# Division on GpSimd one slot later, with four rows of numerators and reciprocals, in an attention and MLP kernel

## The chip, the cores and the metric

The kernel runs on one core of a Trainium2 chip. The metric is the device time of one execution in microseconds (us). The profiled execution is one such run, and its trace names the instructions of each engine: PE (TensorE matmuls), PEld (its weight loads), DVE (VectorE), ACT (ScalarE), POOL (GpSimd) and SP (SyncE, which here only issues DMAs).

## The reference

```python
def _attn_ref(q, k, v, w_phi):
    def phi(x):
        proj = np.einsum('bhsd,df->bhsf', x, w_phi)
        proj = proj - np.max(np.abs(proj), axis=-1, keepdims=True)
        return np.concatenate([np.exp(proj), np.exp(-proj)], axis=-1)
    q_p, k_p = (phi(q), phi(k))
    kv = np.einsum('bhsf,bhsd->bhfd', k_p, v)
    z = np.sum(k_p, axis=2)
    num = np.einsum('bhsf,bhfd->bhsd', q_p, kv)
    den = np.einsum('bhsf,bhf->bhs', q_p, z)[..., None] + 1e-06
    return (num / den).astype(np.float32)

def _moe_ref(x, w_in, w_out, alpha):
    h = x @ w_in
    g = np.maximum(h, 0.0) + alpha * np.minimum(h, 0.0)
    return (g @ w_out).astype(np.float32)
```

The attention has 8 batches of 8 heads, 576 positions and 64 dimensions. Its output, turned to 4608 tokens by 512, goes through the two matrix products of the MLP (512 to 2048 to 512). All is float32.

## The kernel before

The first third of the run is the attention. Two heads make a pair, and there are 32 pairs. `places(i)` (L61) gives every step of pair i a time in slots, counted from slot i; all steps of all pairs are sorted by that time, and the order is kept on each engine's queue (PE, SP, DVE, ACT and POOL). So one slot of the steady state holds the late steps of one pair, the middle steps of the next, the early steps of those behind them, and the decoding of one block of the MLP's weights.

The steps around the change, with the place in slots of an ordinary pair i:

- `k_sum` (i + 0.0055, L406 and L407, POOL): two additions that make `y`, from which PE takes the sum of the key features in `k_z` (i + 1.0035, L433).
- `num` and `den` (i + 2.0013 and i + 2.004, PE, L522 and L541) read the exponentials of the queries, `qf`, which ACT wrote at i + 1.39 to 1.46 (L507, L510). ACT copies the numerators to a row `s` (i + 2.002, L534) and the denominators to `ds` (i + 2.0065, L551).
- `den_out` (i + 2.025, SP, L555) reads `ds` back in a small layout; `invert` (i + 2.7825, DVE, L559) takes the reciprocals; `rec_out` (i + 2.785, SP, L562) writes them to DRAM; `spread` (i + 3.027, SP, L567) reads them back, broadcast over the partitions, into a row `r`. It can only be issued when the write has landed.
- `finish` (i + 3.1, POOL, L572) multiplies `s` by `r`, and `store` (i + 3.8, SP, L575) writes the product to `x_d`, the input of the MLP.

The decoding of a weight block (`stages`, L178 to L239) runs between them: SP loads `raww` (L182), ACT scales (L191, L193), DVE takes the sign and joins (L200, L204), POOL adds (`decode_add`, L208), ACT halves (L148), DVE subtracts (L151) and SP stores (L238, L239). On POOL one slot is thus `y`, `y`, `finish`, add. On SP one slot is: the weight stores, `den_out`, `spread`, the weight load, the load of v (L329), the load of q and k (L325), `rec_out`, `store` of the pair before.

Buffers: `qf` has two of 9216 bytes per partition (`QH_BUFS`); `s` rotates among two in the pool `st` and one in `wk`; `r` has two in `st`. For the first four pairs ACT and DVE split the quotient into two parts (`first_x`, L657, at X0T + i), which are the first operands of the MLP.

After the last pairs (time T2, L723) the order by hand holds for PE, SP and POOL alone. The MLP's first column of tokens follows, then pairs of columns by a fast product with seven multiplications, in which `g_tiles` (L953) takes the two `qf` buffers for its units 0 and 1.

Of the kernel before, what the change touches and what calls it, by code (L numbers as in the profile page):

```python
# [8 lines left out]
F32 = mybir.dt.float32  # L9
# [8 lines left out]
P = 128  # L18
B, H, S, D = 8, 8, 576, 64
# [4 lines left out]
NPAIR = B * NP  # L24
# [8 lines left out]
C2 = 512  # L33
# [19 lines left out]
X_BUFS = 2  # L53
RAW_BUFS = 2
S_BUFS = 2
QH_BUFS = 2
NHALF = 1
NBURST = 3

# [1 line left out]
def places(i):  # L61
    end = i >= NPAIR - 2
    first = {}
    if i < NBURST:
        first = dict(
            ld=-1.9, lv=-0.45, p=(-0.9955, -0.2197), pl=-1.034 if i == 2 else -0.2217, ke=(-0.1643, -0.0202), y=0.0055
        )
    if i == 0:
        first |= dict(
            kz=0.965, ka=0.6934, ko=0.967, kr=1.1197, kc=1.4241, s0=1.9, s=1.91,  # L70
            d=1.77, ds=1.78, n=1.8361, q=(0.96, 0.9362, 0.4904), qe=(0.9994, 1.0, 0.968),
        )
    if i == 1:
        first |= dict(y=0.1, ka=0.003, kz=0.12, ko=0.43, kr=1.002)
    return dict(
        ld=-2.217,
        lv=-1.96,
        p=(-0.2197, -0.219),
        pl=-0.2185,
        dr=-0.218,  # L80
        ke=(-0.19, 0.0046),
        kz=1.0035,
        ka=1.0012,
        ko=1.0045,
        kr=1.0191,
        kc=1.1461,
        q=(1.4089, 1.41 if i == NPAIR - 1 else 1.4543, 1.3558),
        qe=(1.4364, 1.4627, 1.3892),
        d=2.004,
        ds=2.0065,  # L90
        n=2.0013,
        s0=2.002,
        s=2.0043,
        d9=2.025,
        dv=2.7825,
        rd=2.785,
        rr=3.027,
        x=6.75 if end else 3.1,
        xs=6.76 if end else 3.8,
        y=0.0055,  # L100
    ) | first


W = dict(load=-1.9212, sign=-0.1262, scale=-0.1512, split=-0.1196, add=-0.1112, high=0.8388, low=0.8674, store=1.0588)
W0 = dict(load=-1.3, sign=-0.9513)
X0T = 4.47
X0L = 0.363
HEADS = (31.9, 32.3, 32.62, 32.9)
T2 = 33.05
# [17 lines left out]
def fused_kernel(ctx: ExitStack, tc: tile.TileContext, kq, v, w_phi, w_in, w_out, alpha, out):  # L127
# [155 lines left out]
    qp = ctx.enter_context(tc.tile_pool(name="qp", bufs=2))  # L283
    wdq = ctx.enter_context(tc.tile_pool(name="wdf", bufs=2))
    st = ctx.enter_context(tc.tile_pool(name="st", bufs=2))
# [14 lines left out]
    wk = att.enter_context(tc.tile_pool(name="wk", bufs=3))  # L300
# [12 lines left out]
    for n in range(2):  # L313
        k4 = cat.tile([P, 2, 2, FD], F32, name=f"k4_{n}")
        pool.memset(k4[64:P], 0.0)
        k4buf.append(k4)

    def attention_units(i):
        b, hp = divmod(i, NP)
        c = {}  # L320
# [180 lines left out]
        def q_exp(h):  # L501
            ps = None if halved and h == 2 else c["qt", h]
            if h == 2:
                c["qf"] = qp.tile([P, 2, 2, S], F32, tag="qf", name=f"qf{i}", bufs=QH_BUFS)
            for a, sg in enumerate((1.0, -1.0)):
# [23 lines left out]

        def num_out(u):  # L530
            if u == 0:
                own = i % 3 == 2 and i < NPAIR - 2
                c["s"] = (wk if own else st).tile([P, S], F32, tag="s", name=f"s{i}", bufs=1 if own else S_BUFS)
            act.copy(c["s"][:, u * HS : (u + 1) * HS], c["n", u])  # L534

        def den():
# [25 lines left out]
            nc.sync.dma_start(rec_d[i].rearrange("(p j) -> p j", j=36), c["d9"])  # L562

        def spread():
            c["r"] = st.tile([P, S], F32, tag="r", name=f"rr{i}", bufs=2)
            for h in range(2):
                nc.sync.dma_start(  # L567
                    c["r"][h * D : (h + 1) * D], rec_d[i : i + 1, h * S : (h + 1) * S].broadcast_to([D, S])
                )
# [4 lines left out]
        def store():  # L574
            nc.sync.dma_start(x_d[hp, :, b * S : (b + 1) * S], c["r"])  # L575

        at = places(i)
        us = [
            (at["ld"], load),
# [7 lines left out]
            (at["n"], num),  # L587
            (at["d"], den),
            (at["s0"], lambda: num_out(0)),
            (at["s"], lambda: num_out(1)),  # L590
            (at["ds"], den_copy),
            (at["d9"], den_out),
            (at["dv"], invert),
            (at["rd"], rec_out),
            (at["rr"], spread),
            (at["x"], finish),
            (at["xs"], store),
# [39 lines left out]
    xs, po = {}, {}  # L637
# [19 lines left out]
    def first_x(j, rows):  # L657
# [8 lines left out]

        return [(X0T + j, cast), (X0T + X0L + j, rest)]

# [12 lines left out]
    def down_tile(name, dtype):  # L681
        return wdq.tile([P, 2, 2, WN], dtype, tag="wd", name=name, bufs=2 * NPRE)
# [237 lines left out]
    end = t1 + (len(order) - HEAD) * U2 - 0.002  # L920
# [30 lines left out]
        dve.scalar_tensor_tensor(g, r, al1[:, ff : ff + 1], src, op0=ALU.mult, op1=ALU.add)  # L951

    def g_tiles(p, u):  # L953
        if u < 2:
            t = qp.tile([P, 2, 2, S], F32, tag="qf", name=f"g_{p}_{u}", bufs=QH_BUFS)
            return {(r, c): t[:, r, c, :C2] for r in range(2) for c in range(2)}
        if u < 4:
            t = [down_tile(f"g_{p}_{u}_{r}", F32).rearrange("p c t w -> p c (t w)") for r in range(2)]
            return {(r, c): t[r][:, c] for r in range(2) for c in range(2)}
        if u == NU - 1:  # L960
            tag = lambda r, c: (st, [P, S], "sr"[r])
        else:
            tag = lambda r, c: (late["gs"], [P, C2], f"g{u}{r}{c}")
        g = {}
        for r in range(2):
            for c in range(2):
                q, shape, t = tag(r, c)
                g[r, c] = q.tile(shape, F32, tag=t, name=f"g_{p}_{u}_{r}{c}", bufs=2 if u == NU - 1 else 1)[:, :C2]
        return g
# [3 lines left out]
    def unit(p, u):  # L973
# [17 lines left out]
        def rest():  # L991
            g = g4[p, u] = g_tiles(p, u)
            if fresh:
                added(g[0, 0], st["b"], st["p1"])
            leaky(g[0, 0] if fresh else st["b"], g[0, 0], f1, f"11_{tag}")
            product(st["a"], p, u, S2, False, False)
            st["u2"] = copied(st["a"], f"u2_{tag}")
            st["c"] = bank(1, f"pc{tag}")
            product(st["c"], p, u, S1, True, False)
            p5 = copied(st["c"], f"p5_{tag}")  # L1000
            product(st["a"], p, u, S3, False, False)
            added(g[1, 1], st["a"], p5)
# [196 lines left out]
```

## Time and profile before

| | us |
|---|---|
| runs, not profiled (3): median | 989.25 |
| their lowest and highest | 985.78, 989.32 |
| the profiled execution | 985.83 |
| its span, first to last instruction | 984.0 |
| PE busy | 958.2 (97%) |
| DVE busy | 758.2 (77%) |
| ACT busy | 632.9 (64%) |
| POOL busy | 255.3 (26%) |

The shares are means over two very different parts. Up to about 310 us the attention keeps PE, DVE, ACT, POOL and the DMA engines all busy; from about 360 us to the end the MLP is a stream of matmuls. POOL's 255 us lie almost all in the first part. The granted clock of TensorE is 1.00 of full speed in every slice.

### The profile page before, as it was taken

What the parts mean: (1) busy time and instruction counts of PE and PEld (TensorE: products, weight loads), DVE (VectorE), ACT (ScalarE), POOL (GpSimd) and SP (SyncE); (2) the same over time, 40 slices, a digit from 0 to 9 for tenths busy, and PEclk for the clock granted to TensorE, in tenths of its full rate; (3) what the DMA queues carried; (4) which work ended last, traced back from release to release, by engine and by line L of the source; (5) the groups of instructions that cost most, each with busy time, mean ns of one, the idle gap of its engine ahead of it and who ended that gap; (6) DMA issues with size and microseconds to landing.
All of it is one profiled execution on the core that took longest, in us unless ns stands there. A gap on an engine that the chain in (4) does not pass through costs nothing.

```text
span 984.0 us, 19065 instructions
## 1 busy us (share of the span) xinstructions
PE 958.2 (97%) x7152; PEld 787.0 (80%) x7152; DVE 758.2 (77%) x1186; ACT 632.9 (64%) x1207; POOL 255.3 (26%) x222
## 2 busy tenths in 40 slices
PE   8999999989998999999999999999999999999998
PEld 6766667666675888888888888888888888888887
DVE  6899988887887499788988366987465986565874
ACT  5998989988887456566665455664445664454653
POOL 3567667666666122111001000000000000000001
PEclk9999999999999999999999999999999999999999
DMA  5688888988885789997778566677567676566565
GB/s 196 230 275 309 297 298 321 298 300 308 299 290 207 272 312 379 338 343 275 248 240 259 202 205 242 243 252 259 195 213 248 224 261 231 183 213 204 182 226 180
DMA packets 97611, 252.23 MB, mean 256 GB/s; under 512 B 12464, under 2 KB 13104, under 8 KB 97520
## 3 DMA queue, kind: packets, MB, share of 16 engines
q1 hardware_dynamic: 87088, 215.42, 64.8%
q0 software_dynamic: 10000, 35.39, 9.4%
q8 instruction: 57, 0.93, 0.4%
q14 instruction: 34, 0.28, 0.1%
q10 hardware_dynamic: 432, 0.20, 0.1%
HBM read 189.87 MB, written 60.96 MB: 255 GB/s over the span
## 4 chain that ended last, share of the span: by engine, by line
PE 61%; DVE 3%; DMA 2%; issue 1%; ACT 1%; POOL 0%; SPq 0%; ACTq 0%; DVEq 0%; POOLq 0%
PE qa L931 6%; PE qa L932 6%; PE qa L930 6%; PE pa L930 5%; PE pa L932 5%; PE pa L931 5%; PE qc L931 3%; PE qc L932 3%; PE qc L930 3%; PE pc L932 3%; PE pc L930 3%; PE pc L931 3%; PE qb L930 1%; PE qb L932 1%; PE qb L931 1%; PE pb L932 1%
## 5 line engine op out<-in xcount | busy, mean ns | idle before, releaser
L144 ACT CAST hv<-g 128x512 fp32r<-128x512 f32 x224 | 136.4, 619 | 91.7 <-PE qa L932 45.3
L154 DVE TENSOR_TENSOR hv<-g,hv 128x512 fp32r<-128x512 f32 x224 | 150.4, 685 | 40.3 <-ACT hv L144 39.1
L808 POOL DMA_DIRECT2D out_dram<-pt x35 | 18.9, 541 | 500.6 <-ACT pt L1098 429.3
L932 PE MATMUL qa<-hv,wv 128*128 128x512 f32 (+1 forms) x257 | 97.3, 379 | 0.0
L931 PE MATMUL qa<-hv,wv 128*128 128x512 f32 (+1 forms) x257 | 97.3, 379 | 0.0
L930 PE MATMUL qa<-hv,wv 128*128 128x512 f32 (+1 forms) x257 | 97.3, 379 | 0.0
L406 POOL TENSOR_TENSOR y<-xk 128x1024 f32<-128x1024 f32 x32 | 76.2, 2380 | 10.1 <-ACT xk L400 10.1
L400 ACT ACTIVATE xk<-t 128x1024 f32<-128x1024 f32 (+1 forms) x66 | 64.3, 1025 | 8.5 <-DVE t L386 8.5
L572 POOL TENSOR_TENSOR rr<-s,rr 128x576 f32<-128x576 f32 x32 | 49.5, 1548 | 75.5 <-DMA rr<-rec_d 36.7
L950 ACT ACTIVATE r<-g 128x512 f32<-128x512 f32 x65 | 37.4, 621 | 44.4 <-DVE g L946 44.4
L522 PE MATMUL n<-qf,sf 128*64 128x288 f32 x464 | 61.5, 407 | 2.9 <-DVE t L386 2.9
L419 PE MATMUL kv<-xk,v 128*64 128x256 f32 x512 | 62.3, 386 | 0.7 <-ACT ks L443 0.7
L385 DVE TENSOR_REDUCE m<-pj 128x8 f32<-128x1024 f32 (+2 forms) x38 | 43.2, 1136 | 25.1 <-PE pj L375 25.1
L510 ACT ACTIVATE qf<-qt 128x512 f32<-128x512 f32 x116 | 60.6, 639 | 0.0
L951 DVE SCALAR_TENSOR_TENSOR g<-r,al,g 128x512 f32<-128x512 f32 x65 | 45.9, 747 | 18.8 <-ACT r L950 18.8
L932 PEld LDWEIGHTS qa<-hv,wv 128*128 128x128 f32 x257 | 48.7, 190 | 6.8
L931 PEld LDWEIGHTS qa<-hv,wv 128*128 128x128 f32 x257 | 48.7, 189 | 6.8
L930 PEld LDWEIGHTS qa<-hv,wv 128*128 128x128 f32 x257 | 48.7, 189 | 6.7
L522 PEld LDWEIGHTS n<-qf,sf 128*64 128x64 f32 x464 | 34.0, 137 | 24.6 <-ACT aw L191 4.9
L154 DVE TENSOR_TENSOR xo<-xr,xo 128x512 fp32r<-128x512 f32 x56 | 40.5, 736 | 15.0 <-ACT xo L144 14.7
L144 ACT CAST xo<-xr 128x512 fp32r<-128x512 f32 x56 | 33.8, 619 | 25.7 <-DVE xr L859 12.6
L986 ACT COPY pb<-pa 128x512 f32<-128x512 f32 x31 | 17.7, 570 | 50.6 <-PE pa L932 50.0
(210 smaller groups left out, 2713.3 us busy)
## 6 DMA issues: line engine op xcount, KB each, us to landing
wv<-vs_d SPq DMA_DIRECT2D x64, 512.0 KB
ws<-us_d SPq DMA_DIRECT2D x54, 512.0 KB
wv<-v_d SPq DMA_DIRECT2D x48, 512.0 KB
wa<-u_d SPq DMA_DIRECT2D x37, 512.0 KB
raw<-kq_dram SPq DMA_DIRECT2D x31, 576.0 KB
v<-v_dram SPq DMA_DIRECT2D x32, 320.0 KB
rr<-rec_d SPq DMA_DIRECT2D x64, 144.0 KB
x_d<-rr SPq DMA_DIRECT2D x32, 288.0 KB
```

Source lines behind the costliest of these rows:

```text
L144: return act.copy(dst, src)
L154: return eng.tensor_tensor(dst, src, f(hi), op=ALU.subtract)
L400: act.activation(x[:, a, :, js], c["t", 0][:, :, js], AF.Exp, scale=sg)
L406: pool.tensor_tensor(y, x[:, :, : 2 * FD], x[:, :, 2 * FD :], op=ALU.add)
L419: pe.matmul(c["kv"][h * D : (h + 1) * D, 0:2], lhsT=c["v"][:, tp, h, :], rhs=c["x", ch][:, :, h, j, :], start=tp == 0, stop=tp == NV - 1,)
L510: act.activation(dst, ps, AF.Exp, scale=sg)
L522: pe.matmul(ps[h * D : (h + 1) * D, :], lhsT=c["st"][:, a, h * D : (h + 1) * D], rhs=c["qf"][:, h, a, u * HS : (u + 1) * HS], start=a == 0 ...
L572: pool.tensor_tensor(c["r"], c["s"], c["r"], op=ALU.mult)
L930: pe.matmul(ps, lhsT=wh, rhs=xh, start=first, stop=False, skip_group_check=True)
L931: pe.matmul(ps, lhsT=wl, rhs=xh, start=False, stop=False, skip_group_check=True)
L932: pe.matmul(ps, lhsT=wh, rhs=xl, start=False, stop=end, skip_group_check=True)
L951: dve.scalar_tensor_tensor(g, r, al1[:, ff : ff + 1], src, op0=ALU.mult, op1=ALU.add)
```

## The change

The division of a pair moves from i + 3.1 to i + 4.1 and its store from i + 3.8 to i + 4.8, for all but the last two pairs. The broadcast read moves from i + 3.027 to i + 3.05, which on SP puts it behind the weight load (slot fraction 0.03) and the load of v (0.04). The splits for the first four pairs move one slot later (X0T). Since a row now lives a slot longer, numerators and reciprocals have four rows each: two in `st` and two single tiles in the pool `qp`, which take the room of the second `qf` buffer. In the MLP unit 1 of `g_tiles` uses these four rows.

```diff
-QH_BUFS = 2
+QH_BUFS = 1
@@ def places(i):
-        rr=3.027,
-        x=6.75 if end else 3.1,
-        xs=6.76 if end else 3.8,
+        rr=3.05,
+        x=6.75 if end else 4.1,
+        xs=6.76 if end else 4.8,
@@
-X0T = 4.47
+X0T = 5.47
@@ def fused_kernel(...):
+    def row(kind, i):
+        if i % 4 > 1:
+            return spare(f"{kind}{i % 4}", f"{kind}{i}")
+        return st.tile([P, S], F32, tag=kind, name=f"{kind}{i}", bufs=2)
+
+    def spare(tag, name):
+        return qp.tile([P, S], F32, tag=tag, name=name, bufs=1)
@@ def num_out(u):
-                own = i % 3 == 2 and i < NPAIR - 2
-                c["s"] = (wk if own else st).tile([P, S], F32, tag="s", name=f"s{i}", bufs=1 if own else S_BUFS)
+                c["s"] = row("s", i)
@@ def spread():
-            c["r"] = st.tile([P, S], F32, tag="r", name=f"rr{i}", bufs=2)
+            c["r"] = row("r", i)
@@ def g_tiles(p, u):
+        if u == 1:
+            return {(r, c): spare(f"{'sr'[r]}{2 + c}", f"g_{p}_{u}_{r}{c}")[:, :C2] for r in range(2) for c in range(2)}
```

## Rows read from the trace of the kernel before

**Rows 1.** Windows, three stretches: length, busy us (instructions) by engine, clock, DMA share, GB/s.

```profile
40.00:100.00 60.00, 57.73 (x816) 40.28 (x816) 57.48 (x83) 56.10 (x118) 42.89 (x26) 1.00 0.84 288
100.00:300.00 200.00, 187.48 (x2708) 132.11 (x2702) 172.03 (x256) 177.17 (x380) 134.26 (x84) 1.00 0.88 302
300.00:363.00 63.00, 60.16 (x367) 47.85 (x358) 43.37 (x66) 34.65 (x71) 23.49 (x24) 1.00 0.72 256
```

**Rows 2.** Groups by line, POOL, 99 to 310 us: busy us, mean ns | idle before.

```profile
L406 POOL TENSOR_TENSOR y<-xk 128x1024 f32<-128x1024 f32 x22 | 52.4, 2384 | 0.0
L572 POOL TENSOR_TENSOR rr<-s,rr 128x576 f32<-128x576 f32 x23 | 35.5, 1544 | 64.9 <-DMA rr<-rec_d 29.6 <-DVE ew L200 12.4 <-DVE aw L204 7.8
L407 POOL TENSOR_TENSOR y<-y 128x512 f32<-128x512 f32 x23 | 29.7, 1291 | 1.8
L208 POOL TENSOR_TENSOR aw<-cw,aw 128x512 int32<-128x512 int32 x22 | 28.0, 1273 | 2.0 <-ACT qf L510 2.0
```

**Rows 3.** Waits, 100 to 310 us, of PE (all) and ACT's longest: total, times, longest.

```profile
PE kv L433 <- POOL y L407: 10.4, 12, 2.0
PE n L522 <- DVE t L386: 1.3, 1, 1.3
PE m L375 <- ACT qf L507: 0.6, 1, 0.6
...
ACT raww L148 <- POOL aw L208: 15.7, 16, 2.2
```

**Rows 4.** Timeline of PE, the first matmuls on `y` of some pairs: start, us.

```profile
99.53 0.43 PE L433 MATMUL kv<-y,ones 128*32 128x128 f32 x8 [0.25 <-POOL y L407]
...
126.73 0.43 PE L433 MATMUL kv<-y,ones 128*32 128x128 f32 x8 [0.33 <-POOL y L407]
137.05 0.43 PE L433 MATMUL kv<-y,ones 128*32 128x128 f32 x8 [1.44 <-POOL y L407]
145.85 0.43 PE L433 MATMUL kv<-y,ones 128*32 128x128 f32 x8
...
288.31 0.42 PE L433 MATMUL kv<-y,ones 128*32 128x128 f32 x8
298.94 0.43 PE L433 MATMUL kv<-y,ones 128*32 128x128 f32 x8 [1.76 <-POOL y L407]
```

**Rows 5.** Timeline of POOL, 205 to 216 us.

```profile
205.04 1.87 POOL L572 TENSOR_TENSOR rr<-s,rr 128x576 f32<-128x576 f32 x1 [4.61 <-DMA rr<-rec_d]
206.88 1.28 POOL L208 TENSOR_TENSOR aw<-cw,aw 128x512 int32<-128x512 int32 x1
...
215.15 1.41 POOL L572 TENSOR_TENSOR rr<-s,rr 128x576 f32<-128x576 f32 x1 [3.31 <-DMA rr<-rec_d]
```

**Rows 6.** Timeline of SP, DMA issues, 197 to 214 us.

```profile
197.05 0.60 SPq L555 DMA_DIRECT2D d<-ds  x1
...
203.75 0.33 SPq L562 DMA_DIRECT2D rec_d<-d  x1
206.94 0.33 SPq L575 DMA_DIRECT2D x_d<-rr  x1
...
210.44 1.67 SPq L567 DMA_DIRECT2D rr<-rec_d  x2
...
213.78 0.37 SPq L562 DMA_DIRECT2D rec_d<-d  x1
```

**Rows 7.** Timeline of DVE, ACT and POOL, single rows.

```profile
203.35 0.37 DVE L559 RECIPROCAL d<-d 32x36 f32<-32x36 f32 x1 [2.25 <-DMA rr<-rec_d]
204.95 0.69 DVE L204 SCALAR_TENSOR_TENSOR aw<-aw,ew 128x512 uint32<-128x512 uint32 x1
213.65 0.39 ACT L551 ACTIVATE ds<-m 128x288 f32<-128x288 f32 x1
...
262.82 1.43 POOL L572 TENSOR_TENSOR rr<-s,rr 128x576 f32<-128x576 f32 x1 [3.55 <-DMA rr<-rec_d]
263.06 1.74 DVE L204 SCALAR_TENSOR_TENSOR aw<-aw,ew 128x512 uint32<-128x512 uint32 x1
```

## The prediction, made before the change was built

> **What bounds the kernel now.** I read four views in this order. The windows first: in the attention's steady part, 100 to 300 us, PE is busy 187.48 of 200 us, ACT 177.17, DVE 172.03 and POOL only 134.26 [rows 1]. By busy time POOL looks like the engine with most room, and that is the trap of this case.
>
> Second, the groups of POOL. Of its four steps per slot only the division waits: 64.9 us of idle time stand before its 23 instances, next to nothing before the others [rows 2]. Per slot POOL works 2.384 + 1.291 + 1.544 + 1.273 = 6.49 us and waits 64.9 / 23 = 2.82 us before the division, together 9.31 us. (The releaser is the broadcast read; the DVE lines named with it can't be, since the division reads only `s` and `r`.)
>
> Third, the slots by PE: the first matmul on `y` comes at 99.53 and, 21 slots later, at 298.94 [rows 4]. That is 9.50 us per slot. POOL's 9.31 us nearly fill it: POOL is never free, though a third of its time is waiting.
>
> Fourth, the waits show who pays. PE waits 10.4 us for `y`, and ACT 15.7 us for POOL's addition of the decoded weights; PE's other waits are 1.3 + 0.6 us [rows 3]. The queue on POOL is in order, so the division's wait is handed to `y` and to the addition behind it.
>
> The wait is also a loop. The division that starts at 205.04 ends at 206.91; SP then issues its store at 206.94 [rows 5, 6]. Behind that store on SP stand the weight stores, the denominators' read and the next broadcast, issued at 210.44, whose data releases the next division at 215.15 [rows 5, 6]. One turn is 215.15 - 205.04 = 10.11 us. The broadcast has a second condition, the landing of the reciprocals written at 203.75, 6.69 us before [rows 6].
>
> What would the slot be without POOL? A slot in which PE waits for nothing on `y` is 145.85 - 137.05 = 8.80 us [rows 4]; I take 8.81, to which several others come within 0.02. The excess of the 21 slots is 199.41 - 21 x 8.81 = 14.4 us. After 300 us PE has 63.00 - 60.16 = 2.8 us idle up to 363 us, and between 40 and 100 us it has 2.3 [rows 1].
>
> **The change, part by part.**
>
> *The division one slot later.* The count of instructions stays. The division now multiplies by a row that was issued almost a slot before: it is released when the second `y` ends. POOL's slot falls from 9.31 to 6.49 us of work, 2.3 below PE's 8.81. The addition behind it goes at the end of DVE's join instead of the end of the division: at 204.95 + 0.69 = 205.64 instead of 206.88 [rows 5, 7], 1.24 us earlier in this slot, and `y` with it. With POOL no longer a queue late, that grows until `y` waits for nothing but its exponentials.
>
> *The store one slot later.* SP issues it when the division is long done, so the weight stores, the denominators' read and what is behind them no longer wait for POOL. In the slot shown the store could be issued right after the reciprocals' write at 203.75 instead of at 206.94 [rows 6], so the denominators' read comes up to 3 us earlier for DVE.
>
> *The broadcast behind two loads.* It passes the weight load and the load of v on SP. These no longer stand behind its wait for the reciprocals, and SP's loop from one write of reciprocals to the next (213.78 - 203.75 = 10.03 us, of which 6.69 are the landing [rows 6]) loses their issue time. The broadcast now also stands behind v's wait for its buffer. It took 215.15 - 210.44 = 4.71 us to release the division [rows 5, 6]; behind two loads it may take several more, but it now has a whole slot more, 8.8 us. Cost: nothing; if that cover were gone, the division would wait again, for the overshoot.
>
> *One buffer of query exponentials.* ACT may write the next pair's `qf` only when PE's `num` and `den` have read the last. On ACT the copy of the denominators (at 213.65 [rows 7]), which needs `den` finished, stands before these exponentials in the same slot, so the wait is already met. Cost: nothing, and if ACT did wait, it would be no longer than this copy waits now. The rows of `s` and `r` come round after four slots and are held for under three. The casts of the first four pairs move with the division; unit 1 of `g_tiles` takes the new rows long after the last store. No cost.
>
> *The end of the attention.* Pair 29's division falls behind T2; it stays before the next DMA issue on POOL and after the last addition, which therefore no longer waits for the broadcast. PE has only 2.8 us idle there [rows 1]. I bound this part by -2 and +2.8 us and take 0, since PE is 95% busy; between 40 and 100 us DVE is busy 57.48 of 60 us, so I take 0 there also, with 2.3 us as the other end [rows 1].
>
> *The sum.* Excess 14.4 us, less PE's waits that have nothing to do with POOL (1.9 us [rows 3]): 12.5 us gained. Against the profiled execution this is 985.83 - 12.5 = 973.3 us. The median of the runs lies 989.25 - 985.83 = 3.4 us above that execution, so 976.8 us. What is late next is PE itself, with ACT at 177.17 / 200 x 9.50 = 8.4 and DVE at 8.2 us per slot close behind [rows 1]; their jitter can eat some. I put the gain of this case at 8 to 15 us.
>
> **A rule against the change.** A division that runs beside DVE's join makes the join 1.74 us instead of 0.69 [rows 7], 1.05 us more. The Trainium skill, GPSIMD Engine Reference, section 8 (Key points), says that GpSimd shares its SBUF interfaces with VectorE and contends with instructions that have two SBUF inputs; the trace agrees, 1.74 against 0.69. By that page the place of the division against DVE's three such steps (L151, L200, L204) decides, and the rival below is what it would do here.
>
> **The rivals.**
>
> *B. The round trip stays the bound.* Five of the 21 slots take over 10.3 us, from the one that ends at 137.05 (10.32) to the one that ends at 298.94 (10.63) [rows 4]; together they are 53.8 us, 9.8 above the floor. In one of them the denominators' read, issued at 197.05, holds DVE's reciprocal until 203.35, 6.30 us later, with 2.25 us of idle time on DVE [rows 6, 7]. If these trips and not POOL make the long slots, they stay: the gain is 12.5 - 9.8 = 2.7 us, 986.5 us. Against it: the read was late because the store before it stood behind the division. By the Trainium skill (DMA: Bandwidth & Descriptors, Anatomy of one DMA) a small transfer takes about 2.0 us, and this rival would be gone; the rows show 6.30 and 6.69 us, and they decide.
>
> *C. All goes to the floor*, the stretch from 40 to 100 us too: 14.4 + 2.3 = 16.7 us, 972.5 us. For it: the division beside DVE's steps also lengthens that stretch. Against it: DVE is nearly full there.
>
> *D. Slower: the division lands on DVE's steps.* DVE works 172.03 / 200 x 9.50 = 8.17 us per slot [rows 1]. If POOL's new order puts `y` or the division beside two of the three steps in each slot, DVE comes to 8.17 + 2 x 1.05 = 10.27 us: 21 x (10.27 - 9.50) = 16 us more, 1005 us. It decides from 9.50 - 8.17 = 1.33 us of stretch per slot on. Against it: the division would start right after `y`, some 5 us after the join (1.27 of addition and 3.68 of `y` [rows 2]) and end at 6.5, while the next three steps begin about 2 us before the next join at 8.8.
>
> *E. It doesn't do what it says:* the broadcast, behind two loads, lands after the `y` of the next slot, and POOL waits as before. No change, 989 us. It needs 4.71 + 8.8 = 13.5 us or more from issue to release, where 4.71 were seen.
>
> **How the numbers follow.** Forecast 0.62, B 0.16, C 0.07, D 0.07, E 0.08. The predicted time is the forecast's, 976.8 us. The range goes from 970.5 (C with 2 us from the end of the attention) to 987.0, just past B's centre; it leaves out D, E and a part of B. About 0.5% (5 us) is what a measurement of this kernel can tell from no change. Faster: forecast, C and a little of B, 0.72. Within: the rest of B, and E, 0.21. Slower: D, 0.07.
>
> **What would show each step.** In the profile after: the division's idle time before it goes from 64.9 to under 5 us; PE's wait for `y` and ACT's for the addition nearly vanish; SP issues the store with no wait for POOL; the first matmuls on `y` come 8.8 to 9.0 us apart, the long slots gone; DVE's join keeps 0.69 us. B would show as reciprocals or broadcasts that still wait for landings over 6 us, with slots over 10 us left; D as L151 and L204 well over 1 us; E as idle time before L572 that stays. A forecast that fails otherwise would have PE at 8.8 in the attention and the gain given back between 300 and 363 us.

## The result, and the profile after

The changed kernel takes 973.35 us (median of 4 runs, 969.33 to 974.84) against 988.08 us before (4 runs, 985.78 to 989.32): a ratio of 0.9847 with a 95% interval of 0.981 to 0.9885, or 14.7 us. Run again beside three others it gave 0.9863 (0.9839 to 0.9888). The forecast was 976.8 us, with a range of 970.5 to 987.0. The profiled execution took 972.53 us, with a span of 970.7 us; the one of before took 985.83 us with 984.0.

The windows of the changed kernel, with the columns of [rows 1] (length, busy us of PE, PEld, DVE, ACT and POOL with instructions, clock, DMA share, GB/s):

```profile
40.00:100.00 60.00, 60.00 (x875) 42.20 (x873) 56.39 (x87) 58.58 (x128) 41.88 (x27) 1.00 0.98 306
100.00:300.00 200.00, 197.97 (x2781) 139.81 (x2778) 175.62 (x261) 183.20 (x395) 141.97 (x90) 1.00 0.97 314
300.00:363.00 63.00, 60.43 (x298) 50.68 (x296) 47.81 (x84) 33.60 (x65) 17.05 (x25) 1.00 0.80 279
```

PE is busy 197.97 of 200 us where it was 187.48, and all of the 60 us before that. The DMA engines, at 0.88 before, are now at 0.97.

POOL's groups from 99 to 310 us, as [rows 2] (L579 is now the division):

```profile
L414 POOL TENSOR_TENSOR y<-xk 128x1024 f32<-128x1024 f32 x22 | 52.5, 2384 | 0.0
L579 POOL TENSOR_TENSOR r<-s,r 128x576 f32<-128x576 f32 x24 | 35.3, 1472 | 1.5 <-DMA r<-rec_d 1.5
L208 POOL TENSOR_TENSOR aw<-cw,aw 128x512 int32<-128x512 int32 x24 | 31.3, 1303 | 58.4 <-ACT qf L515 38.1 <-ACT qf L518 16.7 <-PE qt L457 2.1
L415 POOL TENSOR_TENSOR y<-y 128x512 f32<-128x512 f32 x22 | 28.5, 1295 | 1.7
```

The idle time before the division fell from 64.9 to 1.5 us. POOL still stands idle for 58 us, now before the addition, which needs DVE's join (the exponentials `qf` named in the row are not an input of it). That idle time is room: nobody waits for it, as the waits of 100 to 310 us show (total, times, longest):

```profile
DVE d L566 <- DMA d<-ds: 6.2, 6, 1.9
...
ACT raww L148 <- POOL aw L208: 2.7, 6, 0.5
...
PE kv L441 <- POOL y L415: 0.8, 3, 0.4
```

PE's wait for `y` went from 10.4 to 0.8 us and ACT's for the addition from 15.7 to 2.7 [rows 3]. The first matmuls on `y`, from PE's timeline, for some pairs of the changed kernel:

```profile
52.83 0.43 PE L441 MATMUL kv<-y,ones 128*32 128x128 f32 x8
...
96.86 0.43 PE L441 MATMUL kv<-y,ones 128*32 128x128 f32 x8
...
193.73 0.43 PE L441 MATMUL kv<-y,ones 128*32 128x128 f32 x8
202.54 0.43 PE L441 MATMUL kv<-y,ones 128*32 128x128 f32 x8
...
238.26 0.43 PE L441 MATMUL kv<-y,ones 128*32 128x128 f32 x8 [0.28 <-POOL y L415]
248.38 0.42 PE L441 MATMUL kv<-y,ones 128*32 128x128 f32 x8 [0.38 <-POOL y L415]
...
284.58 0.43 PE L441 MATMUL kv<-y,ones 128*32 128x128 f32 x8 [0.17 <-POOL y L415]
```

From 52.83 to 202.54 us every slot takes 8.81 us, the floor of the forecast. After that a few long ones are left, the longest 10.12 us (248.38 - 238.26).

Where the time came from: the pair that stood at 298.94 us [rows 4] now stands at 284.58, 14.4 us earlier. Its 21 slots before it took 199.41 us and now take 284.58 - 96.86 = 187.72, 11.7 us less. The five slots in front of those took 99.53 - 52.16 = 47.37 us (the row of before is shown below) and now 44.03, 3.3 us less. The start is 0.7 us later. From that pair to the end of the span it is 984.0 - 298.94 = 685.1 us before and 970.7 - 284.58 = 686.1 now, so that 13.3 us of the lead are left. The loss at the start and the one at the end are both within the spread of the runs, 5.5 us.

```profile
52.16 0.43 PE L433 MATMUL kv<-y,ones 128*32 128x128 f32 x8
```

The 3.3 us go with DVE, which was busy 45.88 of those 47.37 us. Its groups by form, first of the kernel before (52 to 99.5 us), then of the changed one (52 to 97 us); the mean ns stands before the second bar:

```profile
L204 DVE SCALAR_TENSOR_TENSOR aw<-aw,ew 128x512 uint32<-128x512 uint32 x5 | 5.5, 1108 | 0.5
L151 DVE SCALAR_TENSOR_TENSOR wd<-aw,wd 128x512 fp32r<-128x512 f32 x3 | 4.2, 1414 | 0.0
```

```profile
L204 DVE SCALAR_TENSOR_TENSOR aw<-aw,ew 128x512 uint32<-128x512 uint32 x5 | 3.5, 693 | 0.5
...
L151 DVE SCALAR_TENSOR_TENSOR wd<-aw,wd 128x512 fp32r<-128x512 f32 x3 | 1.8, 616 | 0.0
```

The join went from 1108 to 693 ns and the subtraction from 1414 to 616, 4.4 us in all: in this stretch the old division ran beside them.

### The profile page after: what moved, and what is told of

It reads as the page before. It is cut to its first block, busy times and chain, and to the rows that moved or that the text cites. A ratio compares the mean times of both kernels' runs of the same rounds, so it can differ in the third digit from the quotient of the medians.

```text
span 970.7 us, 19113 instructions
## 1 busy us (share of the span) xinstructions
PE 957.9 (99%) x7152; PEld 787.1 (81%) x7152; DVE 750.6 (77%) x1186; ACT 630.8 (65%) x1207; POOL 251.7 (26%) x222
## 4 chain that ended last, share of the span: by engine, by line
PE 59%; issue 4%; DVE 3%; ACT 1%; POOL 1%; DMA 1%; POOLq 0%; ACTq 0%; DVEq 0%
PE qa L937 6%; PE qa L939 6%; PE qa L938 6%; PE pa L937 5%; PE pa L938 5%; PE pa L939 5%; PE qc L937 3%; PE qc L938 3%; PE qc L939 3%; PE pc L939 3%; PE pc L937 3%; PE pc L938 3%; PE qb L938 1%; PE qb L937 1%; PE qb L939 1%
## 5 line engine op out<-in xcount | busy, mean ns | idle before, releaser
L208 POOL TENSOR_TENSOR aw<-cw,aw 128x512 int32<-128x512 int32 x32 | 42.4, 1325 | 86.2 <-ACT qf L515 49.8
```

## The experiments

The theory was the forecast's: the division's wait for its broadcast, handed on by POOL's queue, was what held the slots. The rivals were SP's order (the broadcast's move alone), the loop through the store, the new buffers, and the ports that POOL and DVE share. All ratios are against the kernel before, run beside them on the same chip; it took 984.5, 985.1 and 985.3 us there. The edits are given against the changed kernel.

**The buffers alone.**

```diff
-rr=3.05, x=4.1, xs=4.8, X0T = 5.47
+rr=3.027, x=3.1, xs=3.8, X0T = 4.47
```

> The new rows and the one buffer of query exponentials alone: division, store, broadcast and casts keep the places they had before. Theory (the division's wait for its broadcast on POOL is what the change removes): no gain, 988 us within 3, 60 to 65 us of idle time before the division, slots of 9.5 us. Rival 1 (one buffer of query exponentials costs ACT a wait): over 991 us, and ACT rows that wait for the numerators' or denominators' matmuls. Rival 2 (the gain comes from the rows' places or count): under 984 us.

Measured 984.51 us, ratio 1.0002 (0.9986 to 1.0019); POOL's row has 60.6 us of idle time before the division:

```profile
L579 POOL TENSOR_TENSOR r<-s,r 128x576 f32<-128x576 f32 x23 | 34.4, 1498 | 60.6 <-DMA r<-rec_d 46.5 <-DVE ew L200 4.1 <-DMA raww<-w_in_dram 3.1
```

One buffer of query exponentials costs nothing, and four rows alone bring nothing.

**The division late, the broadcast in its old place.**

```diff
-rr=3.05,
+rr=3.027,
```

> The changed kernel with the broadcast in its old place on SP, ahead of the two loads. Theory: the division's place is what counts, 972 to 976 us, under 5 us of idle time before the division. Rival (SP's order gave a good part of the gain): 978 us or more, with slots over 10 us in the second half of the attention.

Measured 990.72 us, ratio 1.0056 (1.0035 to 1.0077). The theory as it stood falls: this is a little slower than the kernel before, though POOL does what it was meant to:

```profile
L579 POOL TENSOR_TENSOR r<-s,r 128x576 f32<-128x576 f32 x22 | 31.3, 1425 | 0.0
...
L208 POOL TENSOR_TENSOR aw<-cw,aw 128x512 int32<-128x512 int32 x22 | 28.0, 1271 | 73.5 <-ACT qf L518 58.0 <-PE pj L383 12.8 <-PE qt L457 2.6
```

No division waits. SP's timeline shows what took its place (issues; start, us):

```profile
165.57 0.37 SPq L569 DMA_DIRECT2D rec_d<-d  x1
...
167.97 0.60 SPq L562 DMA_DIRECT2D d<-ds  x1
171.95 1.56 SPq L574 DMA_DIRECT2D r<-rec_d  x2
173.56 0.58 SPq L182 DMA_DIRECT2D raww<-w_in_dram  x1
174.18 0.43 SPq L337 DMA_DIRECT2D v<-v_dram  x1
174.71 0.38 SPq L333 DMA_DIRECT2D raw<-kq_dram  x1
175.19 0.37 SPq L569 DMA_DIRECT2D rec_d<-d  x1
```

The reciprocals are written at 165.57; SP reaches the broadcast soon after 168.6 and stands there until they have landed, at 171.95, 6.38 us after the write. Behind it wait three loads, which then go out together, right ahead of the next write at 175.19. One turn is 9.62 us, longer than PE's 8.81. In all, SP waits here for 63.7 us between 100 and 300 us; in the changed kernel it is 8.5 (from the queue's waits):

```profile
SPq L574 <- DMA rec_d<-d: 63.7, 20, 4.2
```

```profile
SPq L574 <- DMA rec_d<-d: 8.5, 15, 1.2
SPq L569 <- DVE d L566: 31.6, 20, 2.6
```

The second row of the changed kernel says what holds the write there: DVE's reciprocals, and no longer SP's own queue. Its timeline for one turn:

```profile
185.96 0.33 SPq L569 DMA_DIRECT2D rec_d<-d  x1
...
191.75 1.10 SPq L574 DMA_DIRECT2D r<-rec_d  x2
193.04 0.45 SPq L333 DMA_DIRECT2D raw<-kq_dram  x1
194.91 0.33 SPq L569 DMA_DIRECT2D rec_d<-d  x1
```

All that stands behind the write is issued by 193.49, 7.53 us after it and so within a slot; then SP waits until 194.91. The write landed after 5.79 us here and after 6.38 in the run above, and two loads are off the loop; which of the two brings more was not tested.

**The same, with the denominators' read ahead of the weight stores.** This tells whether the loop goes through that read or through the reciprocals' write.

```diff
-rr=3.05, d9=2.025,
+rr=3.027, d9=2.008,
```

> The changed kernel with the broadcast back in its old place ahead of the two loads (which alone gave 990.7 us), and the denominators' read ahead of the two weight stores. Theory 1 (the loop on SP runs through the write of the reciprocals: 6.4 us until it lands, then the broadcast and the three loads that stand behind it, over 3 us, then the next write): the read's place doesn't cut it, 984 to 991 us, slots of 9.5 us or more. Theory 2 (the loop runs through the denominators' read, slow behind the stores): 971 to 978 us, slots of 8.8 us.

Measured 989.07 us, ratio 1.004 (1.0019 to 1.0062), so theory 1: DVE's wait for the read halves, from 28.6 to 15.1 us, but SP's for the reciprocals stays (100 to 300 us):

```profile
SPq L574 <- DMA rec_d<-d: 69.5, 21, 4.2
```

**The broadcast behind the loads, the division in its old place.**

```diff
-x=4.1, xs=4.8, X0T = 5.47
+x=3.1, xs=3.8, X0T = 4.47
```

> The new rows, and of the moves only the broadcast behind the two loads; division, store and casts keep their old places. Theory: the division still waits, now for a broadcast that is issued behind two loads; 988 to 995 us, idle time before the division 65 us or more. Rival (SP's order gave the gain, since the loads no longer stand behind the wait for the reciprocals): 978 to 983 us.

Measured 1037.93 us, ratio 1.0549 (1.0508 to 1.0591). The direction is the theory's, but the size is far beyond its 995 us. POOL, 99 to 310 us:

```profile
L579 POOL TENSOR_TENSOR r<-s,r 128x576 f32<-128x576 f32 x19 | 26.8, 1411 | 100.5 <-DMA r<-rec_d 84.9 <-DVE t L394 6.3 <-DVE m L393 4.8
```

Here the loop of the forecast is whole and longer: the store at 161.33 us waits for the division; behind it stand the weight stores, the denominators' read, two loads and the broadcast (165.88), which releases the next division at 172.13, whose store goes at 173.57: 12.2 us a turn. TensorE's clock falls as well: from 126 to 130 us PE is busy for 0.82 of 4 us, and from 130 to 132 the granted clock is 0.50 (1.2 of 2.4 GHz) before it comes back; on the mean of 100 to 300 us it is 0.94, against 1.00 before. What that costs beside the loop was not separated.

**The store alone late.**

```diff
-rr=3.05, x=4.1, X0T = 5.47
+rr=3.027, x=3.1, X0T = 4.47
```

> The new rows, and of the moves only the store one slot later; the division keeps its old place, so that it waits for its broadcast, but SP's queue no longer stands behind the division. Theory in its loop form (division, store, denominators' read and broadcast behind it, next division): the loop is cut, but not the wait; half the gain, 979 to 983 us, idle time before the division down to 35 to 50 us. Rival 1 (the wait itself is all): 986 to 990 us. Rival 2 (the loop through the store is all): 972 to 976 us.

Measured 997.81 us, ratio 1.011 (1.0054 to 1.0165): none of the three. The loop through the store is cut, and SP runs into the other one at once:

```profile
SPq L574 <- DMA rec_d<-d: 62.3, 19, 4.0
```

The write at 160.28 us has landed at 167.35, 7.07 us later, and the next write follows at 170.49, 10.2 us after the first. POOL waits 74.8 us before its divisions, more than before. So the two loops had shared the same time: in the kernel before, SP waited 32.4 + 13.4 us at the store and only 21.9 for the reciprocals. Why this kernel is slower than the one before, and not equal to it, is not settled; the granted clock, 0.98 on the mean of 100 to 290 us against 1.00, may be a part of it.

**The division in the slot of its broadcast, but behind the addition.**

```diff
-x=4.1,
+x=3.9,
```

> The changed kernel with the division in the same slot as its broadcast, but on POOL behind the addition of the decoded weights and ahead of the next pair's sums; the store stays at its place. If the time that the broadcast gets is what counts: it lands about 5 us after its issue, the addition starts about 6 us after it, so the division waits little (under 15 us in all), and the time is that of the changed kernel within 2 us. If the division must stand behind the sums (so that they come 1.4 us earlier): PE waits for the sums again, 3 us slower or more.

Measured 979.72 us, ratio 0.9942 (0.9923 to 0.9962), 8.7 us slower than the changed kernel beside it (971.07). The broadcast has landed in time, but `y` now stands behind the division (POOL from 99 to 300 us, then PE's wait from 100 to 290):

```profile
L579 POOL TENSOR_TENSOR r<-s,r 128x576 f32<-128x576 f32 x22 | 31.1, 1414 | 0.6 <-ACT qf L518 0.6
...
PE kv L441 <- POOL y L415: 5.6, 12, 0.7
```

So it isn't only a wait that counts: 1.41 us of work between the addition and `y` are already too much. The ports are not the reason: from 40 to 290 us none of DVE's steps L151, L200 and L204 takes over 0.75 us in this run.

**The changed kernel again, and two smaller moves on SP.**

```diff
-d9=2.025,
+d9=2.008,
```

```diff
-rr=3.05,
+rr=3.784,
```

The first is the denominators' read ahead of the weight stores, the second the broadcast behind the load of q and k also.

> The changed kernel once more, unaltered, beside the next three on the same chip, as their measure: 0.985 of the kernel before, within 0.003.

> The changed kernel with the denominators' read ahead of the two weight stores on SP instead of behind them. What is late in the changed kernel is DVE's reciprocal, which waits 6.2 us in all for this read in the second half of the attention. Theory (the read is slow because of what SP issued just ahead of it): with 768 KB fewer ahead these waits go under 2 us, the long slots after 200 us shrink, 1 to 3 us faster than the changed kernel. Rival (the read takes its time whatever is ahead of it): no change within 1 us.

> The changed kernel with the broadcast also behind the load of q and k, just ahead of the next write of reciprocals. Theory (SP's wait for the reciprocals holds back loads, which then go out in a burst ahead of the next denominators' read): one load fewer in the burst, the same time as the changed kernel or up to 3 us faster. Rival (the broadcast now comes too late for the division one slot later): idle time before the division over 10 us, slower by 3 us or more.

Measured: the changed kernel 971.07 us (970.79 to 971.37), the read first 970.55 (969.02 to 971.88; ratio 0.9857, 0.9831 to 0.9884), the broadcast last 969.03 (968.37 to 969.89; ratio 0.984, 0.9811 to 0.987). The read first does to the profile what was expected: DVE no longer waits for it, and PE has no gap from 100 to 290 us; its row, then that of the changed kernel's second run:

```profile
100.00:290.00 190.00, 190.00 (x2717) 134.49 (x2715) 168.35 (x255) 178.86 (x386) 136.55 (x87) 1.00 1.01 324
```

```profile
100.00:290.00 190.00, 189.02 (x2695) 133.65 (x2694) 167.36 (x253) 178.61 (x386) 134.29 (x86) 1.00 1.00 322
```

That is 1 us, and the runs can't tell it from none. With the broadcast last the slowest of 4 runs is faster than the fastest of 4 of the changed kernel beside it, by 2 us on the median. That is likely a gain, but not a sure one: the first 4 runs of the changed kernel went from 969.33 to 974.84. All the divisions together wait 1.5 us between 99 and 300 us.

**More work on POOL beside DVE.** A second product of the same size behind each division (pairs 0 to 27), and three memsets in its place:

```diff
             pool.tensor_tensor(c["r"], c["s"], c["r"], op=ALU.mult)
+            if i < 28:
+                e = wk.tile([P, S], F32, tag="e", name=f"e{i}", bufs=1)
+                pool.tensor_tensor(e, c["s"], c["r"], op=ALU.mult)   # or: pool.memset(e, float(n)), n in 0, 1, 2
```

> The changed kernel with a second product of the same size behind each division on POOL, written to a tile that nobody reads (pairs 0 to 27). It measures POOL's room and the cost of POOL beside DVE's join. POOL has 2.5 us free per slot, the product takes 1.4. Theory (room only): 971 us within 1.5. Rival (the extra product now runs beside L151, L200 or L204 and lengthens one by 1.05 us per slot; DVE has 0.6 us free): L151 or L204 well over 1 us, slots of 9.2 us, 979 to 985 us.

> The same with three memsets of the tile in the product's place: about the same time on POOL, but nothing read. If POOL's time alone cost something, the result is that of the extra product. If it is the reading of two operands beside DVE's steps: L151 and L204 keep 0.62 and 0.69 us, and 971 us within 1.5.

Measured: the product 993.52 us (ratio 1.0078, 1.0048 to 1.0109), the memsets 971.8 us (ratio 0.986, 0.9822 to 0.9897). POOL's second product and DVE's groups beside it, then POOL's and DVE's with the memsets (99 to 300 us):

```profile
L582 POOL TENSOR_TENSOR e<-s,r 128x576 f32<-128x576 f32 x21 | 37.2, 1773 | 1.6
...
L200 DVE SCALAR_TENSOR_TENSOR ew<-raww 128x512 uint32<-128x512 uint32 x21 | 38.6, 1840 | 0.0
...
L151 DVE SCALAR_TENSOR_TENSOR raww<-aw,raww 128x512 fp32r<-128x512 f32 x18 | 16.3, 907 | 0.0
```

```profile
L583 POOL MEMSET e<- 128x576 f32 x67 | 38.8, 579 | 2.6
...
L208 POOL TENSOR_TENSOR aw<-cw,aw 128x512 int32<-128x512 int32 x23 | 29.3, 1274 | 15.7 <-ACT qf L515 10.2 <-ACT qf L518 3.1 <-PE pj L383 1.5
...
L200 DVE SCALAR_TENSOR_TENSOR ew<-raww 128x512 uint32<-128x512 uint32 x23 | 17.2, 748 | 0.0
...
L151 DVE SCALAR_TENSOR_TENSOR raww<-aw,raww 128x512 fp32r<-128x512 f32 x20 | 13.7, 685 | 0.0
```

Three memsets, 3 x 579 = 1737 ns a slot and so about as long as the second product's 1773, cost nothing: they fill POOL's room (the idle time before the addition falls from 57.6 us in the changed kernel's second run to 15.7). The product costs 22 us, since DVE's sign step goes from 0.75 to 1.84 us and its subtraction from 0.68 to 0.91. The rival held, with a larger price than it named: two steps of a slot were hit, and the slots are 9.6 us.

**Both moves on SP together.**

```diff
-d9=2.025, rr=3.05,
+d9=2.008, rr=3.784,
```

> The changed kernel with both moves on SP that helped or did no harm: the denominators' read ahead of the weight stores, and the broadcast behind the load of q and k. Theory (all slots at PE's 8.81 us, nothing left to gain in the attention): 967 to 970 us, 0.981 to 0.985 of the kernel before. Rival (the two undo each other): 971 us or more.

Measured 968.99 us (968.43 to 969.67), ratio 0.9831 (0.9801 to 0.9861). The median is the lowest of all, level with the broadcast last alone; the interval overlaps that of the changed kernel's second run (0.9839 to 0.9888), so that a gain over it isn't shown. PE is busy 190.00 of 190 us between 100 and 290 us, so this stretch has no more to give without fewer matmuls.

## Why the prediction was right, and where it wasn't

The time and the sign came out: 14.7 us against 12.5 by the medians, 13.3 between the two profiled executions. Of the mechanism one half was right; the other, SP's loop, was named but left without a price. Some of the agreement is luck in the sum: 3.3 us that were put at 0 made up for 0.8 too few in the steady part, 0.7 at the start and 1.1 at the end. And 976.8 us stands on a median of 989.25, 3.4 us above the profiled execution; the kernel before took 984.5 to 985.3 in the later comparisons, so this offset was spread between runs.

- *POOL's wait* as the bound: right as one of two. Its 64.9 us fell to 1.5, and PE's wait for `y` to 0.8; but with the division moved and the broadcast left in its place, the wait is gone as well and the kernel takes 990.72 us.
- *The floor and the steady part:* 8.81 us per slot, met from 52.83 to 202.54 us; 11.7 us gained where 12.5 were written. What is left above the floor goes with the reciprocals' wait for the denominators' read, 6.2 us on DVE, which the forecast had put under "jitter": with that read first, PE has no gap.
- *From 40 to 100 us:* written as 0 with 2.3 at the other end, measured 3.3. The step that failed is "DVE is busy 57.48 of 60 us, so I take 0": a part of that busy time was itself made by the old division, 1108 against 693 ns and 1414 against 616. Rival C was right there.
- *The end of the attention:* 0 was written, -1.1 came, too small to tell from the runs' spread.
- *One buffer of query exponentials at no cost:* right, 1.0002.
- *The broadcast behind two loads "at no cost":* the sign was right, the weight wasn't seen. The text says that the loads no longer stand behind its wait, and gives it no price. The runs do: without this move the division's move is 0.6% slower than the kernel before, with it 1.4 to 1.5% faster. It is as needed as the division's move. Without it the mechanism of rival B, given 0.16, is what comes, and worse than its sum: 6.2 us slower than the kernel beside it, where B had 2.7 us faster.
- *The loop through the store:* half right. It is there (the broadcast alone makes it 12.2 us long), but cutting it alone gives a slower kernel, because a second loop on SP, from one write of reciprocals over its landing to the next, was as long. The forecast named this loop and its two numbers, 10.03 and 6.69 us [rows 6], but gave it no place among the bounds and no term in the sum. The turn from 205.04 to 215.15 that it read as the store's loop was closed by the landing and not by the store, as one more row of SP in the kernel before shows:

```profile
208.30 0.70 SPq L555 DMA_DIRECT2D d<-ds  x1
```

SP is past the store and all behind it at 209.00, and stands until 210.44 for the reciprocals. (The 2.0 us that rival B takes from the Trainium skill, DMA: Bandwidth & Descriptors, Anatomy of one DMA, are given there for DMAs that GpSimd issues; these go out from SP.)

- *Rival D:* right in mechanism, and nearer than 0.07 suggests. In the changed kernel the division ends just ahead of DVE's subtraction:

```profile
184.09 1.42 POOL L579 TENSOR_TENSOR r<-s,r 128x576 f32<-128x576 f32 x1
...
185.86 0.62 DVE L151 SCALAR_TENSOR_TENSOR raww<-aw,raww 128x512 fp32r<-128x512 f32 x1
```

It ends at 185.51, 0.35 us before 185.86. From 40 to 285 us none of the three DVE steps takes over 0.75 us. Behind that the gap is crossed in the changed kernel too: the subtraction at 292.37 takes 1.47 us and the sign step at 293.76 1.91, beside the last of `y` and the division of 293.25. The extra product crossed the gap in most slots (median of the sign step 1.90 us). By the Trainium skill (GPSIMD Engine Reference, section 8, Key points) POOL contends with DVE instructions that have two SBUF inputs. The trace agrees: the sign step, which reads one SBUF tile as both of its inputs, takes 1.84 us on the mean beside the product, and 0.75 with the memsets, which read nothing.

## What to carry to other kernels

An engine with a quarter of busy time over the run (two thirds in the stretch that counts) can set the pace when its queue is in order and one instruction waits for a round trip: add the wait to the work before you call it free. Look for the same round trip in every queue that it passes: here it closed two loops, one through GpSimd and one through the queue that issues the DMAs, and each move alone made the kernel slower; what helped was to put loads ahead of the waiting issue and, with it, the consumer a slot later. Busy time can be inflated by a neighbour, so a full engine is no proof that a stretch can't get faster.

## What the runs showed of the hardware that I had not expected

A read or write of 4.5 KB, issued just behind loads or stores of a megabyte or more, took 6 to 7 us to land (6.30 and 6.69 us before, 7.07 in the kernel with the store alone late). A product on GpSimd lengthened a DVE step on SBUF by up to 1.2 us (1.90 against 0.67 us), while three memsets of the same tile did nothing to it. DVE's large steps that read PSUM (128x1024) took 1.21 to 1.23 us in the changed kernel, also where `y` ran beside them on GpSimd.
